# Attention steps moved by one chunk in a recurrent memory transformer, and memory transposes in 64-wide tiles

## The chip, the cores and the metric

The kernel runs on one core of one Trainium2 chip. The time is the device time of one execution in microseconds (us), lower is better. A run is given as the median of several executions, and one further execution was taken with the hardware profiler. The engines are called as in the profile: PE is TensorE (matmuls; PEld its weight loads), DVE is VectorE, ACT is ScalarE, POOL is GpSimd, SP is SyncE, which here only issues transfers.

## The reference, cut to what matters

Two independent halves are computed and joined along the last axis. Half A is a gated long convolution over 2048 positions and 1024 channels (done as a discrete Fourier transform by matmuls). Half B is a transformer layer with a recurrent memory, and all that is changed lies in it:

```python
mem = mem0                                  # 8 rows of 1024
for s in range(64):                         # 64 segments of 32 rows
    h = concat([mem, x[32*s:32*s+32]])      # 40 rows
    q, k, v = h @ Wq, h @ Wk, h @ Wv        # 32 heads of 128
    p = softmax(mask(q @ k.T * scale))      # memory columns are open, the rest causal
    o = (p @ v) @ Wo                        # 40 rows of 1024
    mem, out[s] = o[:8], o[8:]
```

Every segment needs the memory rows that the segment before it produced, so the 64 segments follow each other.

## The kernel before

At first half A runs, with matmuls of half B filled in: queries, keys and values of the last 8 rows of every segment, which need no memory, are computed for all segments at once and stored in DRAM (`REC`, `VBD`). Then comes the loop over 64 segments, which is most of the time. It is issued in an order written out by hand (`tc.manual_schedule()`): on each engine the instructions stand in the order in which the code calls them, and each waits for its inputs and buffers.

**Weights.** A chunk is 128 x 2048 bf16 (512 KB). Wq, Wk and Wv are 16 chunks each, Wo 16. Most stay in SBUF. The 14 that don't fit are read again in each segment through a ring of five slots (`wring`): `done(ch)` frees a slot as soon as the matmuls of its chunk have been recorded, and `fetch()` issues the next load on SP's queue (L722). Two further chunks of Wo, `KEPT_A` and `KEPT_B`, are held after the first segment in unused columns of PSUM: VectorE copies them in quarters into small SBUF tiles (`quarter`, `quarter_b`, L795) shortly before the matmuls that read them.

**A segment.** The 32 rows that depend on the memory or are not precomputed (8 of memory, 24 of x) go through six projections, `Proj(m, g)`: m is keys, queries, values; g is the first or second 16 heads. A projection has eight chunks, and a chunk is four matmuls (L938) that work on four column tiles of the array, 32 wide, each with 512 columns. `evac` (L947, ScalarE) copies the result to SBUF. Keys and queries are transposed on TensorE (L885 by 32-wide tiles, L957 by whole 128 x 128 blocks), then follow:

- `scores(g, ...)` (L963, L966) into the PSUM tile `SB`;
- `softmax_a` (row maximum L972 and difference L974 on VectorE, masks put back into SB L908 and L909 on VectorE, exponentials L977 on ScalarE);
- `softmax_b` (VectorE: sums L982, reciprocals and products, transposes L999 and L1000 into `PT`);
- `attend(g, PT, V)` (TensorE, L1007 and L1011) into the PSUM tile `OTp`, from 32-row tiles; `V` is the evacuated value projection;
- `evac_o(g)` (ScalarE, L1019), which copies `OTp` to the SBUF tile `OT`.

The output projection `out_half(hp, f, OT)` (L1029) takes one pair of heads hp and one half f of the columns: four matmuls of 256 columns in tiles 64 wide. `out_proj(hps, OT)` runs pairs for both halves. Pairs 0 to 7 belong to OT0, pairs 8 to 15 to OT1. The KEPT chunks are pairs 9 and 13 and come in quarters (`out_quarter`).

**The seam between segments.** The result goes to the SBUF tile `Y` in two halves of columns (L1118, ScalarE). `fill_mem(hT, Y, half)` turns the memory rows of each half with `turn_tile` (L885) into the PSUM tile `tps`, and VectorE copies them (L892) into the next segment's `rec`, the input of its projections. Half 0 is filled ahead of the last two pairs of output matmuls of the segment; half 1 stands behind the first four chunks of the next segment's first key projection.

**The order around the change** is the one in the code below: V0's projection `pv0`, the second scores, `softmax_a` for the second 16 heads (its exponentials included), three chunks of `pv1`, the first attention and its copy OT0, `softmax_b`, the other five chunks of `pv1`, the output projection of pairs 0 to 4, the second attention and its copy OT1, and pairs 5 to 7 as work ahead of the first user of OT1.

Of the kernel before, what the change touches and what calls it, by code (L numbers as in the profile page):

```python
# [420 lines left out]
def b_kernel(ctx: ExitStack, tc, x, mem0, Wq, Wk, Wv, Wo, outb, n_seg, run_a):  # L421
    nc = tc.nc
# [50 lines left out]
    ident = const.tile([128, 128], BF, name="ident")  # L473
# [263 lines left out]
    with c0p:  # L737
# [16 lines left out]
        for g in range(2):  # L754
# [3 lines left out]
            for tb in range(4):  # L758
                vst = vsts[:, tb] if g == 0 else pair()[:].rearrange("p (c w) -> p c w", c=4)
                for c in range(4):  # L760
                    ps = ps0.tile([128, 512], F32, tag="ps0", name="vb_ps")
                    for kc in range(8):
                        nc.tensor.matmul(ps[:], lhsT=xbt(kc)[:, 16 * tb:16 * tb + 16, :].rearrange("p s t -> p (s t)"),  # L763
                                         rhs=ws[kc][:, c * 512:(c + 1) * 512], start=(kc == 0), stop=(kc == 7))
# [115 lines left out]
        nc.gpsimd.dma_start(rec[:], REC[:, s, :])  # L880
        pend[s] = (rec[:, 0:256].rearrange("p (k t) -> p k t", k=8), rec[:, 256:512], rec[:, 512:768])

    def turn_tile(dst, src):
        for e in range(0, 128, 32):
            nc.tensor.matmul(dst[e:e + 32, :], lhsT=src[:, e:e + 32], rhs=ident[:], start=True, stop=True,  # L885
                             is_transpose=True, tile_position=(0, e))

    def fill_mem(hT, Y, half):
        tp = tps[:, 0, :]
        for j in (2 * half, 2 * half + 1):  # L890
            turn_tile(tp[:, j * 128:(j + 1) * 128], Y[:, j * 128:(j + 1) * 128])
        nc.vector.tensor_copy(  # L892
            hT.rearrange("p (dh j) t -> p dh j t", dh=2)[:, :, 2 * half:2 * half + 2, 0:NM],
            tp.rearrange("p (j dh r) -> p dh j r", j=4, dh=2)[:, :, 2 * half:2 * half + 2, 0:NM])

    with tc.manual_schedule():
# [3 lines left out]
        Y = one.tile([128, 512], BF, tag="PT", name="Y0")  # L900
# [6 lines left out]
        def seed_scores():  # L907
            nc.vector.tensor_copy(S[:, 0:4, :], mask[:, 0:1, :].to_broadcast([128, 4, 40]))  # L908
            nc.vector.tensor_copy(S[:, 4:8, :], mask[:, 1:2, :].to_broadcast([128, 4, 40]))  # L909
# [3 lines left out]
        for s in range(n_seg):  # L913
# [6 lines left out]
            def keys(g):  # L920
                KT = one.tile([128, 4, 4, 40], BF, tag="KT", name="KT")
                nc.gpsimd.tensor_copy(KT[:, :, :, 32:40],  # L922
                                      KBs[:, 128 * g:128 * g + 128].rearrange("p (c i t) -> p i c t", c=4, i=4))
                return KT
# [25 lines left out]
            def transposes(sb, tiles=False):  # L950
                tp = tps[:, 0, :]
                for i in range(4):
                    dst, src = tp[:, i * 128:(i + 1) * 128], sb[:, i * 128:(i + 1) * 128]
                    if tiles:
                        turn_tile(dst, src)
                    else:
                        nc.tensor.transpose(dst, src, ident[:])  # L957
                return tp.rearrange("p (i c r) -> p i c r", i=4, c=4)

            def scores(g, QT, KT):  # L960
                for i in range(4):
                    for c in range(4):
                        nc.tensor.matmul(S[32 * c:32 * c + 32, i, :], lhsT=QT[:, i, c, :], rhs=KT[:, i, c, :],  # L963
                                         start=False, stop=False, skip_group_check=True, tile_position=(0, 32 * c))
                for c in range(4):
                    nc.tensor.matmul(SB[32 * c:32 * c + 32, 160:320],  # L966
                                     lhsT=QBs[:, 128 * g + 32 * c:128 * g + 32 * c + 32], rhs=KT[:, :, c, :],
                                     start=False, stop=True, skip_group_check=True, tile_position=(0, 32 * c))

            def softmax_a():  # L970
                mx = two.tile([128, 8], F32, tag="mx", name="mx")
                nc.vector.tensor_reduce(out=mx[:], in_=S, op=ALU.max, axis=AX.X)  # L972
                E = one.tile([128, 8, 40], F32, tag="E", name="E")
                nc.vector.tensor_tensor(out=E[:], in0=S, in1=mx[:].unsqueeze(2).to_broadcast([128, 8, 40]),  # L974
                                        op=ALU.subtract)
                seed_scores()
                nc.scalar.activation(E[:], E[:], ACT.Exp, scale=scale)  # L977
                return E

            def softmax_b(E):  # L980
                ssum = two.tile([128, 8], F32, tag="ssum", name="ssum")
                nc.vector.tensor_reduce(out=ssum[:], in_=E[:], op=ALU.add, axis=AX.X)  # L982
                nc.vector.reciprocal(ssum[:], ssum[:])
                nc.vector.tensor_tensor(out=ssum[:, 4:8], in0=ssum[:, 4:8], in1=rowhead[:], op=ALU.mult)
                nc.vector.tensor_tensor(out=P_pad[:, 0:4, 0:32], in0=E[:, 0:4, 0:32],
                                        in1=ssum[:, 0:4].unsqueeze(2).to_broadcast([128, 4, 32]), op=ALU.mult)
                own = P_pad[:].rearrange("p b k -> p (b k)")[:, 32:320].rearrange("p (i w) -> p i w", w=72)
                nc.vector.tensor_tensor(out=own[:, 0:4, 0:8], in0=E[:, 0:4, 32:40],
                                        in1=ssum[:, 0:4].unsqueeze(2).to_broadcast([128, 4, 8]), op=ALU.mult)
                nc.vector.tensor_tensor(out=E[:, 4:8, :], in0=E[:, 4:8, :],  # L990
                                        in1=ssum[:, 4:8].unsqueeze(2).to_broadcast([128, 4, 40]), op=ALU.mult)
                nc.vector.tensor_copy(P_pad[:, 4, 32:64].rearrange("p (i t) -> p i t", i=4), E[:, 4:8, 32:40])
                with nc.allow_low_precision("one of the four terms is not zero"):
                    nc.vector.tensor_reduce(out=P_pad[:, 4, 0:32], in_=E[:, 4:8, 0:32].rearrange("p i k -> p k i"),
                                            op=ALU.add, axis=AX.X)
                PT = one.tile([128, 2, 4, 40], BF, tag="PT", name="PT")
                for kb in range(2):
                    ks = slice(32 * kb, 32 * kb + 32)
                    nc.vector.transpose(out=PT[:, kb, :, 0:32], in_=P_pad[:, 0:4, ks])  # L999
                    nc.vector.transpose(out=PT[:, kb, :, 32:40], in_=P_pad[:, 4, ks])  # L1000
                return PT
# [15 lines left out]
            def evac_o(g):  # L1017
                OT = one.tile([128, 4, 4, 40], BF, tag="KT" if g else "QT", name="OT")
                nc.scalar.copy(OT[:], o_view)  # L1019
                return OT  # L1020
# [12 lines left out]
            def out_half(hp, f, OT, stop=False):  # L1033
                w = pieces((3, hp, 0))
                for hh in range(2):
                    project(2 * hp + hh, f, w, OT, stop and hh == 1)
                if f == 1:
                    done((3, hp, 0))

            def out_proj(hps, OT):  # L1040
                for hp in hps:
                    for f in range(2):
                        out_half(hp, f, OT)

            def out_quarter(ch, q, w):
                project(2 * ch[1] + q // 2, q % 2, w, OT1)
# [15 lines left out]
            k1 = k1.run(4).evac()  # L1062
            scores(0, QT0, KT0)
            E0 = softmax_a()
            q1 = Proj(1, 1).run(4)
            KT1 = keys(1)
            nc.scalar.copy(KT1[:, :, :, 0:32], transposes(k1))
            PT0 = softmax_b(E0)
            q1 = q1.run(4).evac()
# [3 lines left out]
            V0 = pv0.run(4).evac()  # L1073
            scores(1, QT1, KT1)
            E1 = softmax_a()
            pv1 = Proj(2, 1).run(3)
            attend(0, PT0, V0)
            OT0 = evac_o(0)
            PT1 = softmax_b(E1)
            pv1.run(5)  # L1080
            if not last:
                load_x(s + 1)
            V1 = pv1.evac()
# [1 line left out]
            for f, hps in enumerate((FIRST, FIRST[-1:] + FIRST[:-1])):  # L1085
                for hp in hps:
                    out_half(hp, f, OT0)
            out_proj((4,), OT0)
            attend(1, PT1, V1)
            OT1 = evac_o(1)  # L1090
            qs = {}
            if s == 0:
                out_proj((5, 6, 7), OT0)
                out_proj((9, 13, 8), OT1)
                steps = {}
            else:
                qs["B", 0], qs["A", 0] = quarter_b(0, "E"), quarter(0, "rot")
                out_proj((5, 6, 7), OT0)
                qs["B", 2] = quarter_b(2, "QT")
                out_quarter(KEPT_B, 0, qs["B", 0])  # L1100
                qs["A", 2] = quarter(2, "E")
                out_quarter(KEPT_A, 0, qs["A", 0])
                qs["A", 1] = quarter(1, "rot")
                out_proj((8,), OT1)
                steps = {(0, 0): [("B", 2), ("B", 1, "QT")], (0, 1): [("A", 2), ("A", 3, "E")],
                         (0, 3): [("A", 1), ("B", 3, "rot")], (1, 0): [("B", 1)], (1, 1): [("A", 3)], (1, 2): [("B", 3)]}
            Y = one.tile([128, 512], BF, tag="PT", name="Y")
# [85 lines left out]
```

## Time and profile before

| | us |
|---|---|
| median of 3 runs | 1822.93 (1816.8 to 1824.99) |
| profiled execution, its own time | 1813.57 |
| its span, first to last instruction | 1811.8 |
| TensorE busy in the span | 1701.8 (94%) |
| VectorE, ScalarE, GpSimd busy | 1010.3, 680.7, 266.7 |
| mean granted TensorE clock | 0.985 |

The profiled execution lies below the median of the runs, and below the fastest of them; a difference is therefore added to each of the two. In the profile, a line of the timeline gives the start, the length (both in us), the engine, the source line with operation and tiles (written <- read), the shape, the number of instructions merged into it, and in brackets how long the engine was idle before it and what it waited for. The ends of matmuls are modelled, so that starts are the surer measure on TensorE. In a line of the windows the columns are the window, its length, the busy time of PE, PEld, DVE, ACT and POOL with instruction counts, the granted clock, the share of time in which DMA engines were busy, and GB/s moved.

### The profile page before, as it was taken

What the parts mean: (1) busy time and instruction counts of PE and PEld (TensorE: products, weight loads), DVE (VectorE), ACT (ScalarE), POOL (GpSimd) and SP (SyncE); (2) the same over time, 40 slices, a digit from 0 to 9 for tenths busy, and PEclk for the clock granted to TensorE, in tenths of its full rate; (3) what the DMA queues carried; (4) which work ended last, traced back from release to release, by engine and by line L of the source; (5) the groups of instructions that cost most, each with busy time, mean ns of one, the idle gap of its engine ahead of it and who ended that gap; (6) DMA issues with size and microseconds to landing.
All of it is one profiled execution on the core that took longest, in us unless ns stands there. A gap on an engine that the chain in (4) does not pass through costs nothing.

```text
span 1811.8 us, 71373 instructions
## 1 busy us (share of the span) xinstructions
PE 1701.8 (94%) x30996; PEld 1000.8 (55%) x31028; DVE 1010.3 (56%) x3391; ACT 680.7 (38%) x1195; POOL 266.7 (15%) x499
## 2 busy tenths in 40 slices
PE   6888996759899999999999999999999999999998
PEld 3443322324566666666666666666666666666665
DVE  9927874201455555555555555555555555555555
ACT  6955651112233333333333333333333333333333
POOL 4003341100111111111111111111111111111111
PEclk9999999889999999999999999999999999999999
DMA  9989889997999999999999999999999999999998
GB/s 340 370 305 305 311 258 320 306 335 210 344 365 361 357 350 360 358 363 353 361 356 358 357 352 360 370 358 360 361 355 362 356 358 366 367 363 356 357 358 300
DMA packets 233070, 623.34 MB, mean 344 GB/s; under 512 B 72802, under 2 KB 72946, under 8 KB 232756
## 3 DMA queue, kind: packets, MB, share of 16 engines
q1 hardware_dynamic: 160948, 550.58, 82.4%
q0 software_dynamic: 17056, 45.13, 7.1%
q10 hardware_dynamic: 54752, 23.07, 4.7%
q8 instruction: 243, 3.98, 0.9%
q14 instruction: 71, 0.58, 0.1%
HBM read 563.63 MB, written 57.67 MB: 343 GB/s over the span
## 4 chain that ended last, share of the span: by engine, by line
PE 77%; DMA 9%; DVE 6%; ACT 4%; issue 3%; ACTq 0%; POOL 0%; SPq 0%; another core or an unknown queue 0%; POOLq 0%; DVEq 0%
PE acc L938 33%; PE yacc L1029 24%; PE kb_ps L622 5%; DMA wring<-WS 4%; PE tps L885 3%; PE tps L957 2%; PE vb_ps L763 2%; ACT OT L1019 2%; DMA REC<-stage 2%; DVE mx L972 1%; DVE E L974 1%; ACT s_sb L247 1%; PE OTp L1007 1%; PE s_ps L245 1%; PE SB L963 1%
## 5 line engine op out<-in xcount | busy, mean ns | idle before, releaser
L1029 PEld LDWEIGHTS <-OT 128*64 128x64 bf16 x8255 | 439.1, 109 | 54.6 <-ACT OT L1019 36.9
L938 PEld LDWEIGHTS <-rec 128*32 128x32 bf16 x12288 | 289.4, 96 | 269.3 <-DVE rec L892 35.2
L947 ACT CAST qkv_sb<-acc 128x512 bf16<-128x512 f32 x384 | 225.1, 586 | 352.2 <-PE acc L938 346.9
L938 PE MATMUL acc<-Wres,rec 128*32 128x512 bf16 x3328 | 240.2, 382 | 2.0 <-issue 1.8
L938 PE MATMUL acc<-wring,rec 128*32 128x512 bf16 x2300 | 229.0, 382 | 8.5 <-DMA wring<-WS 7.3
L1029 PE MATMUL yacc<-Wmore,OT 128*64 128x256 bf16 (+1 forms) x2560 | 220.7, 274 | 0.0
L938 PE MATMUL acc<-Wmid,rec 128*32 128x512 bf16 x3072 | 212.1, 379 | 0.5 <-issue 0.3
L1029 PE MATMUL yacc<-wring,OT 128*64 128x256 bf16 x2448 | 194.9, 273 | 2.7 <-DMA wring<-WS 2.5
L1118 ACT CAST Y<-yacc 128x256 bf16<-128x256 f32 x128 | 47.7, 373 | 269.8 <-DVE quarter_b L795 170.8
L938 PE MATMUL acc<-pw,rec 128*32 128x512 bf16 x1796 | 144.7, 380 | 2.0 <-issue 1.9
L795 DVE TENSOR_SCALAR quarter<-OTp 128x256 int32<-128x256 int32 x252 | 99.9, 418 | 74.3 <-ACT OT L1019 74.3
L1019 ACT CAST OT<-OTp 128x640 bf16<-128x640 f32 x128 | 87.4, 683 | 138.5 <-PE OTp L1011 138.5
L1120 POOL DMA_DIRECT2D out_dram<-Y x128 | 63.9, 503 | 496.3 <-ACT Y L1118 496.0
L892 DVE COPY rec<-tps 128x32 bf16<-128x32 bf16 x128 | 22.4, 175 | 193.6 <-PE tps L885 193.6
L938 PE MATMUL acc<-Wlate,rec 128*32 128x512 bf16 x1536 | 117.3, 379 | 0.1
L1057 DVE COPY KT<-tps 128x512 bf16<-128x512 bf16 x64 | 27.2, 425 | 150.8 <-PE tps L885 150.8
L972 DVE TENSOR_REDUCE mx<-SB 128x8 f32<-128x320 f32 x128 | 63.0, 492 | 78.4 <-PE SB L966 78.4
L880 POOL DMA_DIRECT2D rec<-REC x64 | 36.4, 568 | 453.4 <-PE acc L938 437.9
L977 ACT ACTIVATE E<-E 128x320 f32<-128x320 f32 x128 | 60.1, 469 | 78.3 <-DVE E L974 78.3
L1029 PE MATMUL yacc<-Wlate,OT 128*64 128x256 bf16 x1024 | 79.2, 276 | 6.0 <-issue 0.2
L622 PE MATMUL kb_ps<-XBT,pw 128*128 128x512 bf16 x313 | 81.1, 397 | 2.6 <-DMA pw<-in_B_Wk_dram 1.2
L922 POOL COPY KT<-rec 128x128 bf16<-128x128 bf16 x128 | 38.5, 301 | 253.3 <-PE SB L966 253.3
(224 smaller groups left out, 2627.4 us busy)
## 6 DMA issues: line engine op xcount, KB each, us to landing
wring<-WS SPq DMA_DIRECT2D x831, 512.0 KB, 6.0
wring<-WS SPq DMA_DIRECT2D x64, 384.0 KB, 5.4
rec<-REC POOLq DMA_DIRECT2D x64, 192.0 KB, 5.6
SK<-s_sb SPq DMA_DIRECT2D x16, 512.0 KB, 5.3
SU<-s_sb SPq DMA_DIRECT2D x16, 512.0 KB, 5.6
Kg<-SK SPq DMA_DIRECT2D x32, 256.0 KB, 4.1
Ug<-SU SPq DMA_DIRECT2D x32, 256.0 KB, 5.5
REC<-stage ACTq DMA_DIRECT2D x16, 512.0 KB, 12.9
```

What stands on the lines that cost most here:

```text
L622: nc.tensor.matmul(ps[:], lhsT=ws[kc][:, hl * 128:(hl + 1) * 128], rhs=xbt(kc).rearrange("p s t -> p (s t)"), start=(kc == 0), stop=(kc == 7))
L795: nc.vector.tensor_scalar(out=dst, in0=src, scalar1=0, scalar2=None, op0=ALU.bitwise_or)
L885: nc.tensor.matmul(dst[e:e + 32, :], lhsT=src[:, e:e + 32], rhs=ident[:], start=True, stop=True, is_transpose=True, tile_position=(0, e))
L922: nc.gpsimd.tensor_copy(KT[:, :, :, 32:40], KBs[:, 128 * g:128 * g + 128].rearrange("p (c i t) -> p i c t", c=4, i=4))
L938: nc.tensor.matmul(self.acc[32 * c:32 * c + 32, :], lhsT=hT[:, ch[1], :], rhs=w[:, 512 * c:512 * c + 512], start=(ch == chs[0]), stop=(ch ...
L947: nc.scalar.copy(sb[:], self.acc[:])
L972: nc.vector.tensor_reduce(out=mx[:], in_=S, op=ALU.max, axis=AX.X)
L977: nc.scalar.activation(E[:], E[:], ACT.Exp, scale=scale)
L1019: nc.scalar.copy(OT[:], o_view)
L1029: nc.tensor.matmul(yacc[f][64 * dh:64 * dh + m, x - o:y - o], lhsT=lhsT, rhs=r, start=(h == (0, 2 * FIRST[-1])[f] and x == o), stop=stop, ...
L1118: nc.scalar.copy(Y[:, 256 * f:256 * f + 256], yacc[f][:, 0:256])
L1120: nc.gpsimd.dma_start(bass.AP(outb.tensor, outb.offset + SEG * s * 2048 + 512 * dh, [[2048, 32], [1, 512]]), Y[64 * dh + NM:64 * dh + 40, :])
```

## The change

Three edits. `turn_tile` gets a width, and half 0 of the memory is turned with four matmuls in tiles 64 wide instead of eight in tiles 32 wide; half 1 stays as it is. The exponentials leave `softmax_a` for a function of their own; for the first 16 heads they stay where they were, for the second 16 they are issued behind the first attention's copy OT0, and the first attention stands behind two chunks of `pv1` instead of three. The second attention stands behind pair 5 of the output projection instead of pair 4, so that pairs 6 and 7 are left between it and the first user of OT1.

```diff
-    def turn_tile(dst, src):
-        for e in range(0, 128, 32):
-            nc.tensor.matmul(dst[e:e + 32, :], lhsT=src[:, e:e + 32], rhs=ident[:], start=True, stop=True,
+    def turn_tile(dst, src, w=32):
+        for e in range(0, 128, w):
+            nc.tensor.matmul(dst[e:e + w, :], lhsT=src[:, e:e + w], rhs=ident[:], start=True, stop=True,
                              is_transpose=True, tile_position=(0, e))
 
     def fill_mem(hT, Y, half):
         tp = tps[:, 0, :]
         for j in (2 * half, 2 * half + 1):
-            turn_tile(tp[:, j * 128:(j + 1) * 128], Y[:, j * 128:(j + 1) * 128])
+            turn_tile(tp[:, j * 128:(j + 1) * 128], Y[:, j * 128:(j + 1) * 128], 32 if half else 64)
...
                 seed_scores()
+                return E
+
+            def softmax_exp(E):
                 nc.scalar.activation(E[:], E[:], ACT.Exp, scale=scale)
-                return E
...
             E0 = softmax_a()
+            softmax_exp(E0)
             q1 = Proj(1, 1).run(4)
...
             E1 = softmax_a()
-            pv1 = Proj(2, 1).run(3)
+            pv1 = Proj(2, 1).run(2)
             attend(0, PT0, V0)
             OT0 = evac_o(0)
+            softmax_exp(E1)
             PT1 = softmax_b(E1)
-            pv1.run(5)
+            pv1.run(6)
...
-            out_proj((4,), OT0)
+            out_proj((4, 5), OT0)
             attend(1, PT1, V1)
             OT1 = evac_o(1)
             qs = {}
             if s == 0:
-                out_proj((5, 6, 7), OT0)
+                out_proj((6, 7), OT0)
                 out_proj((9, 13, 8), OT1)
                 steps = {}
             else:
                 qs["B", 0], qs["A", 0] = quarter_b(0, "E"), quarter(0, "rot")
-                out_proj((5, 6, 7), OT0)
+                out_proj((6, 7), OT0)
                 qs["B", 2] = quarter_b(2, "QT")
                 out_quarter(KEPT_B, 0, qs["B", 0])
                 qs["A", 2] = quarter(2, "E")
                 out_quarter(KEPT_A, 0, qs["A", 0])
```

## The prediction

> **What bounds the kernel now.** I read the page first (busy time, slices, chain of waits), then the windows of the attention part, then the timeline of one undisturbed segment, since the change moves steps of 0.2 to 0.7 us that no total shows.
>
> ```profile
> PE 1701.8 (94%) x30996; PEld 1000.8 (55%) x31028; DVE 1010.3 (56%) x3391; ACT 680.7 (38%) x1195; POOL 266.7 (15%) x499
> PE 77%; DMA 9%; DVE 6%; ACT 4%; issue 3%; ACTq 0%; POOL 0%; SPq 0%; another core or an unknown queue 0%; POOLq 0%; DVEq 0%
> 1472.00:1638.80 166.80, 165.99 (x3660) 105.89 (x3659) 95.52 (x360) 60.26 (x112) 21.58 (x48) 1.00 0.98 364
> ```
>
> TensorE sets the end: 94% busy, 77% of the chain. The third line is a window of eight segments that nothing disturbed: 166.80 / 8 = 20.85 us each, TensorE busy 99.5% of it, the stream of weights at 364 GB/s. From the second copy into Y of the first segment (475.2 us) to that of the last (1807.5) the 63 segments take 21.15 us on average. So 20.85 is the floor of TensorE's own queue, and 0.30 per segment (19 us in all) is lost to late ring loads and to pauses that the profile calls issue. What the change costs must be read from TensorE's queue inside a clean segment. The first attention, in its timeline:
>
> ```profile
> 1482.68 0.59 ACT L947 CAST qkv_sb<-acc 128x512 bf16<-128x512 f32 x1 [0.46 <-PE acc L938]
> 1482.79 0.60 PE L938 MATMUL acc<-Wres,rec 128*32 128x512 bf16 x8
> 1483.33 0.27 PE L1007 MATMUL OTp<-PT,qkv_sb 32*128 32x40 bf16 x16
> 1483.44 0.23 PE L1011 MATMUL OTp<-PT,VBs 32*128 32x160 bf16 x4
> 1483.60 0.62 PE L938 MATMUL acc<-Wres,rec 128*32 128x512 bf16 x8
> 1483.88 0.47 ACT L977 ACTIVATE E<-E 128x320 f32<-128x320 f32 x1 [0.60 <-DVE E L974]
> 1484.25 0.67 ACT L1019 CAST OT<-OTp 128x640 bf16<-128x640 f32 x1
> 1484.26 0.60 PE L938 MATMUL acc<-Wres,rec 128*32 128x512 bf16 x8
> 1484.47 0.48 DVE L982 TENSOR_REDUCE ssum<-E 128x8 f32<-128x320 f32 x1
> 1484.98 0.30 PE L1029 MATMUL yacc<-Wlate,OT 128*64 128x256 bf16 x2
> ```
>
> The reader is to see two queues. On ScalarE the copy of V0 (L947) ends at 1483.27 and the attention starts 0.06 later; then the second exponentials (L977) stand ahead of the copy OT0 (L1019). On TensorE a chunk of four projection matmuls goes by in 0.215 us, start to start, when nothing waits, so the last two of pv1 end their issue at 1484.26 + 0.43 = 1484.69, and the output projection starts only at 1484.98, when OT0 (to 1484.92) is there. The second attention:
>
> ```profile
> 1486.84 0.17 DVE L1000 STREAM_TRANSPOSE PT<-P_pad 128x32 bf16<-128x32 bf16 x1
> 1487.28 0.27 PE L1007 MATMUL OTp<-PT,qkv_sb 32*128 32x40 bf16 x16
> 1487.74 0.69 ACT L1019 CAST OT<-OTp 128x640 bf16<-128x640 f32 x1 [2.18 <-PE OTp L1011]
> 1488.46 0.42 DVE L795 TENSOR_SCALAR quarter<-OTp 128x256 int32<-128x256 int32 x1 [1.15 <-ACT OT L1019]
> 1488.90 0.28 PE L1029 MATMUL yacc<-quarter_b,OT 128*64 128x256 bf16 x2
> 1489.01 0.28 PE L1029 MATMUL yacc<-quarter,OT 128*64 128x256 bf16 x2
> ```
>
> A chain hangs on this attention: OTp, the copy OT1 on ScalarE, behind it (1.15 us idle) the copy "quarter" of kept weights out of the same OTp on VectorE, and its use at 1489.01, only 0.13 after it ended (1488.88). Last, Y's transposes between output matmuls:
>
> ```profile
> 1491.84 0.27 PE L1029 MATMUL yacc<-B_rest,OT 128*64 128x256 bf16 x2
> 1491.90 0.22 PE L1029 MATMUL yacc<-quarter_b,OT 128*64 128x128 bf16 x1
> 1492.05 0.29 PE L885 MATMUL tps<-ident,Y 128*32 128x128 bf16 x8
> 1492.28 0.41 PE L1029 MATMUL yacc<-Wring,OT 128*64 128x256 bf16 x4
> 1492.45 0.17 DVE L892 COPY rec<-tps 128x32 bf16<-128x32 bf16 x1 [1.27 <-PE tps L885]
> 1492.83 0.40 PE L938 MATMUL acc<-wring,rec 128*32 128x512 bf16 x4
> ```
>
> **The price of a change of tile shape.** Output matmuls go by at 0.0545 us each. The row ahead of the second attention (four of them from 1486.97) would end its issue at 1487.19; the attention starts at 1487.28 though PT1 was ready at 1487.01. The first projection at 1492.83 follows four from 1492.52 (to 1492.74), and its rec was ready at 1492.62. So going to another tile shape costs 0.09 to 0.10 us with nothing to wait for.
>
> **Part 1, 64-wide transposes.** From 1491.84 the last kept weights, as much as two matmuls of 256 columns, 0.11 of issue, to 1491.95; transposes at 1492.05 (+0.10); eight of them to the next start 0.23, where the second half's eight, between 32-wide projections, take 0.11 (+0.12); the four output matmuls behind them 0.24 instead of 0.22 (+0.02). Four 64-wide tiles hold the same columns, two side by side instead of four, so their issue stays 0.11, and both changes of shape go: gain 0.24. The cover is then thin: transposes at 1491.95 end about 0.30 later, VectorE starts 0.11 behind that (as now), copies 0.17, and TensorE sees it 0.05 later: 1492.58; the projection would be due at 1491.95 + 0.11 + 0.44 + 0.10 = 1492.60. Were the copy late by a few hundredths, that much of the gain goes. The change of shape has no row for 64-wide transposes; between gain 0 and 0.24 I take 0.24, since the second half's rows show no cost of transposing itself.
>
> **Part 2, first attention one chunk earlier.** Two projection chunks stand ahead of it instead of three, so it is due at 1483.00 (1482.79 + 0.215), but V0 lands where it did: it starts at 1483.33 as before. The pause grows from 0.11 to 0.32, or, if the 0.06 behind V0 is chance and the 0.11 only the shape change, not at all. I take the pause: every copy of ScalarE that a matmul waits for is used 0.05 to 0.06 after its end (OT0: 1484.92 to 1484.98). Six chunks follow, 1483.60 + 6 x 0.215 + 0.02 + 0.10 for the shape = 1485.01. OT0 is no longer in the way: the attention's matmuls end at 1483.67, ScalarE takes 0.11 to see it (1487.63 to 1487.74 in the second), copies 0.69, done 1484.47. So 0.19 of waiting goes and 0.215 comes: the projection starts 0.03 later than now.
>
> **Part 3, the second exponentials behind OT0.** They start where the copy's end overlaps them by 0.10, at 1484.38 instead of 1483.88. Their reader L982 stood 0.12 behind their end, held by the second mask copy, so it slips 0.41 only, and with it the whole VectorE chain: PT1 at 1487.42. The second attention, 0.03 later and behind one more pair of heads (8 x 0.0545 = 0.44), is due at 1487.75. Cover 0.33: nothing lost. V1's copy, 0.2 later, still ends before the second half of the columns needs its accumulator.
>
> **Part 4, second attention one pair later.** Its chain moves with it by 0.47, but the users of OT1 and of "quarter" don't: two pairs of heads are left as cover instead of three. OT1: 1487.75 + 0.46 + 0.69 = 1488.90, just in time for quarter_b (due 1487.75 + 0.28 + 0.90 = 1488.93). "quarter" on VectorE: 1488.93 to 1489.35, usable at 1489.40; TensorE is due there at 1489.06. A new pause of 0.34; the matmuls now at 1489.01 start at 1489.40, 0.39 to 0.40 later. The later quarters queue behind on VectorE but slip only 0.17, so they gain cover. Queued behind that pause is all of TensorE: the rest of the output, Y, the next segment's projections. Of ring loads only those released after it (L722, pairs 8 and 14) are issued later.
>
> **Sum.** Per segment +0.40 - 0.24 = +0.16; over 63 segments +10 us. Against this, of the 19 us lost outside the floor some is given back, because a longer period gives each load more time: nothing at least, and at most what TensorE shows as waits for the ring, 7.3 + 2.5 = 9.8 us. I take 2, since such waits come in single bursts of up to 1 us, of which 0.16 buys back little. So +8: the profiled execution from 1813.57 to about 1821.6, the median from 1822.93 to 1831.
>
> **Rivals.**
> Stream-bound (no change, 1823): if the ring, not TensorE, sets the 21.15 average, a floor of 21.01 is still below it and nothing is seen. For it: DMA engines busy 97% to 98%, and 358 GB/s over the window of all 63 segments. Against it: eight segments in a row at 364 GB/s and the same 20.85. It decides from the point where the 0.30 lost per segment falls under 0.16. The Trainium skill, page "DMA: Bandwidth & Descriptors", section "Where 436 GB/s comes from", gives about 358 GB/s as the limit of one core's HBM side; by it a segment's 364 x 20.85 = 7.59 MB would need 21.2 us and the change would move nothing. The trace's mean agrees, its clean window does not.
> The first attention is not held by V0 (1818): it starts at 1483.11, everything behind is 0.21 earlier, and 63 x 0.21 = 13 us come off: 5 us faster than before. It decides if the first attention matmul starts more than 0.06 after V0's copy now because of the shape alone. The even 0.05 to 0.06 behind other ScalarE copies speaks against it.
> Transposes pay for shape at any width (1846): part 1 brings nothing, +15 us on top. The second half's 0.11 for eight speaks against it.
> The order not being as the edit says is excluded: in the built order TensorE, ScalarE and VectorE have these steps in these places, and the "quarter" copy waits for OT1's copy as before.
>
> **How the numbers follow.** Forecast 0.58, stream-bound 0.16, no V0 hold 0.08, no gain from width 0.10, something unlisted 0.08. The forecast's bounds are 1823 (all ring waits given back) and 1836 (none, and rec late by 0.05). The range 1819 to 1843 takes these in and leaves out most of the V0 and width cases. A measurement of this kernel tells about 0.5% (9 us) from no change; 1831 lies just within it, so the forecast gives 0.30 to slower and 0.28 to same; stream-bound and V0 give same 0.21 and faster 0.03; width is slower, 0.10; the unlisted go 0.05 to slower and 0.03 to faster.
>
> **What would show it.** In a clean segment after: period 21.0; first attention 0.05 to 0.06 behind V0's copy, 0.3 after TensorE was free; output projection not waiting for OT; "quarter" matmuls 0.05 behind VectorE's copy, with a TensorE pause of 0.3; transposes next to output matmuls at 0.11. A clean period at or under 20.85, or no pause at "quarter", would prove it wrong.

## The result and the profile after

The changed kernel takes 1830.83 us (median of 7 runs, 1829.04 to 1835.03) against 1820.06 for the kernel before in the same comparison: 11 us slower, ratio 1.0067 with a 95% interval of 1.0048 to 1.0087. The profiled execution took 1830.29 us, its span 1828.4. The forecast was 1831, from +8; the sign and the places were right, and part of the close hit is luck, since the three runs of before that it was added to lie 2 us above the median of 29 (1820.9): the difference itself was forecast as 8 us and measured as 11.

The page and a window of four undisturbed segments of the profile after, to be read against the busy times and the window shown of before:

```profile
PE 1708.5 (93%) x30772; PEld 997.2 (55%) x30772; DVE 1016.6 (56%) x3391; ACT 682.2 (37%) x1195; POOL 265.8 (15%) x499
1223.83:1308.00 84.17, 82.95 (x1816) 52.35 (x1816) 48.18 (x180) 30.26 (x56) 10.74 (x24) 1.00 0.97 359
```

TensorE is still the bound. A clean segment takes 84.17 / 4 = 21.04 us instead of 20.84, though over the whole run 256 matmuls fewer are issued, and TensorE idles 1.4% of it instead of 0.5%. The floor rose by 0.20 us, 63 x 0.20 = 12.6 us. The first attention in the timeline after:

```profile
1255.46 0.59 ACT L947 CAST qkv_sb<-acc 128x512 bf16<-128x512 f32 x1 [0.46 <-PE acc L938]
1255.57 0.39 PE L938 MATMUL acc<-Wres,rec 128*32 128x512 bf16 x4
1256.10 0.27 PE L1009 MATMUL OTp<-PT,qkv_sb 32*128 32x40 bf16 x16
1256.56 0.69 ACT L1021 CAST OT<-OTp 128x640 bf16<-128x640 f32 x1 [0.51 <-PE OTp L1013]
1257.14 0.47 ACT L980 ACTIVATE E<-E 128x320 f32<-128x320 f32 x1
1257.26 0.60 PE L938 MATMUL acc<-Wres,rec 128*32 128x512 bf16 x8
1257.79 0.52 PE L1031 MATMUL yacc<-Wlate,OT 128*64 128x256 bf16 x6
```

V0's copy ends at 1256.05 and the attention starts 0.05 later, as before; but only one chunk lies between 1255.57 and it, so TensorE pauses 0.53 - 0.215 = 0.32 us there. The copy OT0 is done at 1257.25, and the output projection at 1257.79 no longer waits for it: it follows its last eight matmuls by 0.53, which is 0.43 of issue and 0.10 for the change of tile shape. What the free copy gave, the longer pause took. The second attention:

```profile
1260.03 0.17 DVE L1002 STREAM_TRANSPOSE PT<-P_pad 128x32 bf16<-128x32 bf16 x1
1260.53 0.27 PE L1009 MATMUL OTp<-PT,qkv_sb 32*128 32x40 bf16 x16
1260.99 0.69 ACT L1021 CAST OT<-OTp 128x640 bf16<-128x640 f32 x1 [2.44 <-PE OTp L1013]
1261.71 0.43 DVE L795 TENSOR_SCALAR quarter<-OTp 128x256 int32<-128x256 int32 x1 [1.21 <-ACT OT L1021]
1261.73 0.30 PE L1031 MATMUL yacc<-quarter_b,OT 128*64 128x256 bf16 x2
1262.19 0.30 PE L1031 MATMUL yacc<-quarter,OT 128*64 128x256 bf16 x2 [0.16 <-DVE quarter L795]
```

PT1 is ready at 1260.20, 0.33 ahead of the attention: the late exponentials cost nothing here. Behind the attention the chain of copies ends at 1262.14, and the quarter's matmuls start 0.05 later, 0.46 behind those of quarter_b where 0.11 is their issue. The bracket gives 0.16 of idle time, because the ends of matmuls are modelled; the starts give 0.35. The list of TensorE's waits (total in us, how often, the longest in us) has it in all but two of the 63 segments that have quarters, and next the waits for the ring:

```profile
PE yacc L1031 <- DVE quarter L795: 9.6, 61, 0.2
PE acc L938 <- DMA wring<-WS: 8.2, 10, 5.2
```

And the seam:

```profile
1265.03 0.27 PE L1031 MATMUL yacc<-B_rest,OT 128*64 128x256 bf16 x2
1265.14 0.31 PE L885 MATMUL tps<-ident,Y 128*64 128x128 bf16 x4
1265.25 0.41 PE L1031 MATMUL yacc<-Wring,OT 128*64 128x256 bf16 x4
1265.47 0.42 PE L1031 MATMUL yacc<-pw,OT 128*64 128x256 bf16 x4
1265.54 0.17 DVE L892 COPY rec<-tps 128x32 bf16<-128x32 bf16 x1 [1.15 <-PE tps L885]
1265.81 0.40 PE L938 MATMUL acc<-wring,rec 128*32 128x512 bf16 x4
```

Start to start, the last kept weights, the transposes and twice four output matmuls behind them take 0.11, 0.11, 0.22 and 0.34, together 0.78, where it was 0.99 before (1491.84 to 1492.83). Both changes of shape around the transposes are gone. That this is 0.21 and not 0.24 has its cause further up in the segment; the last section comes back to it.

### The profile page after: what moved, and what is told of

Its sections match the earlier page's. It is cut to its first block, busy times and chain, and to the rows that moved or that the text cites. A ratio compares the mean times of both kernels' runs of the same rounds, so it can differ in the third digit from the quotient of the medians.

```text
span 1828.4 us, 70893 instructions
## 1 busy us (share of the span) xinstructions
PE 1708.5 (93%) x30772; PEld 997.2 (55%) x30772; DVE 1016.6 (56%) x3391; ACT 682.2 (37%) x1195; POOL 265.8 (15%) x499
## 4 chain that ended last, share of the span: by engine, by line
PE 76%; DMA 12%; DVE 5%; ACT 4%; issue 2%; POOL 0%; ACTq 0%; SPq 0%; POOLq 0%; DVEq 0%
PE acc L938 36%; PE yacc L1031 20%; DMA wring<-WS 6%; PE kb_ps L622 5%; PE tps L885 3%; PE tps L957 2%; PE vb_ps L763 2%; ACT OT L1021 2%; DMA REC<-stage 2%; DVE mx L972 2%; PE OTp L1009 2%; ACT s_sb L247 1%; DVE quarter L795 1%; PE s_ps L245 1%; DMA KS_nat<-in_A_ssm_k_dram 1%
## 5 line engine op out<-in xcount | busy, mean ns | idle before, releaser
L1031 PE MATMUL yacc<-wring,OT 128*64 128x256 bf16 x2448 | 199.7, 274 | 2.7 <-DMA wring<-WS 2.3
L1031 PE MATMUL yacc<-quarter,OT 128*64 128x256 bf16 x504 | 76.2, 275 | 9.7 <-DVE quarter L795 9.6
```

Source lines behind the costliest of these rows:

```text
L1031: nc.tensor.matmul(yacc[f][64 * dh:64 * dh + m, x - o:y - o], lhsT=lhsT, rhs=r, start=(h == (0, 2 * FIRST[-1])[f] and x == o), stop=stop, ...
```

## The experiments

Times are medians, each against the kernel before in the same comparison; "floor" is the length of a clean segment in the run's trace (with the last segment left out, the shortest fifth agree within 0.01 us). All floors can be compared, since TensorE's granted clock was full in the loop.

| kernel | floor, us | 63 x change of floor | measured | ratio to before, 95% interval |
|---|---|---|---|---|
| before | 20.84 | | 1820.9 | |
| changed | 21.04 | +12.6 | +10.8 | 1.0067 (1.0048 to 1.0087) |
| width_only | 20.605 | -15 | -12.1 | 0.9938 (0.9917 to 0.9959) |
| moves_only | 21.275 | +27 | +21.7 | 1.0123 (1.0098 to 1.0148) |
| three_chunks | 20.83 | -1 | -1.6 | 0.9998 (0.9982 to 1.0015) |
| pair8_first | 20.69 | -9 | -0.4 | 1.0004 (0.9989 to 1.0019) |
| second_unmoved | 20.705 | -8.5 | -0.8 | 0.9993 (0.9973 to 1.0014) |
| three_and_pair8 | 20.48 | -23 | -8.2 | 0.9946 (0.9926 to 0.9967) |
| second_one_more | 21.47 | +40 | +26.4 | 1.0151 (1.0128 to 1.0173) |

### The two halves of the change apart: width_only and moves_only

```diff
 # width_only: the kernel before, with
-            turn_tile(tp[:, j * 128:(j + 1) * 128], Y[:, j * 128:(j + 1) * 128])
+            turn_tile(tp[:, j * 128:(j + 1) * 128], Y[:, j * 128:(j + 1) * 128], 32 if half else 64)
 # moves_only: the changed kernel, with
-            turn_tile(tp[:, j * 128:(j + 1) * 128], Y[:, j * 128:(j + 1) * 128], 32 if half else 64)
+            turn_tile(tp[:, j * 128:(j + 1) * 128], Y[:, j * 128:(j + 1) * 128], 32)
```

> The kernel before with the 64-wide transposes of half 0 alone. Shape theory: two changes of tile shape go, clean segment 20.84 to about 20.63 us (the copy into rec, a few hundredths late, eats a little of the 0.24), so 63 x 0.21 = 13 us faster than before. Rival, stream-bound: the weights set the pace, clean segments may be shorter but the total stays within 3 us of before. Rival, transposes pay at any width: nothing.

> The changed kernel with half 0 turned in 32-wide tiles again, so only the moves of the attentions and of the exponentials. Pause theory: clean segment 21.045 + 0.21 = 21.25 us, 26 us slower than before, with the wait for the quarter copy in every segment. Stream-bound rival: the extra pauses are given back in part by fewer late loads, 15 us slower or less.

Measured: width_only 1808.79 us against 1820.94, floor 20.605, 0.235 less. moves_only 1842.62 us, floor 21.275, 0.43 more. So the 64-wide transposes are a gain of their own, and the moves are the whole loss. Both floors are as foretold to 0.03; of the times, width_only brought 12 of its 15 us and moves_only cost 22 of its 27. The expected loss of a few hundredths to a late copy into rec did not come: the whole 0.235 is there, and as much (21.275 - 21.04) lies between moves_only and the changed kernel.

### The pause at the quarter: pair8_first

```diff
                 qs["A", 2] = quarter(2, "E")
+                out_proj((8,), OT1)
                 out_quarter(KEPT_A, 0, qs["A", 0])
                 qs["A", 1] = quarter(1, "rot")
-                out_proj((8,), OT1)
```

> The changed kernel with pair 8 of the output projection recorded ahead of the first quarter of KEPT_A, so that 0.44 us of other matmuls lie between the second attention's copy chain and its user. Pause theory: the wait of 0.35 us at the quarter goes, clean segment 21.045 - 0.35 = 20.70 us, 9 us faster than before. If the 0.35 were anything else (a change of shape, a ring load of pair 8), it stays: 12 us slower than before.

The floor fell as the pause theory says, 0.35 to 20.69, and the wait for the quarter is gone from the list of TensorE's waits. The time fell by only half of that: 1820.51 us is some 11 us under the changed kernel, where the floor promises 22, and no faster than before (1820.94). What took the place of the pause stands in the same list, of this kernel:

```profile
PE acc L938 <- DMA wring<-WS: 16.9, 18, 5.4
```

16.9 us where the changed kernel waited 8.2. In both, about 6 us of it belong to the first segment; in the other 63, and with the waits in the output projection, it is 11.3 against 2.7. (The execution profiled took 1825.0 us, 4.5 more than the median, so the median may hold fewer of them.) The cause of the pause is shown; that taking it away makes the kernel faster than before is not.

### The first attention and V0: three_chunks

```diff
-            pv1 = Proj(2, 1).run(2)
+            pv1 = Proj(2, 1).run(3)
...
-            pv1.run(6)
+            pv1.run(5)
```

> The changed kernel with the first attention behind three chunks of pv1 again, five behind it; the copy OT0 stays ahead of the second exponentials. V0 theory: the attention starts at the same distance (0.05 us) behind V0's copy as in both kernels, one chunk less follows, clean segment 21.045 - 0.215 = 20.83 us, equal to before within 2 us. If the third chunk is paid wherever it stands: no change from the changed kernel, 12 us slower than before.

1819.34 against 1820.94, floor 20.83: 0.215 less than the changed kernel, as much as one chunk. In its trace the attention starts 0.057 behind V0's copy, as in the other two kernels. So moving the first attention up bought nothing at all: a chunk of waiting ahead of it in exchange for a chunk of work. The part that pays is the order of ScalarE's two instructions, OT0 ahead of the exponentials: with three chunks ahead of the attention in both kernels, the output projection starts 0.17 earlier in the segment here than before.

### The second attention: second_unmoved and second_one_more

```diff
 # second_unmoved: the changed kernel, with
-            out_proj((4, 5), OT0)
+            out_proj((4,), OT0)
...
-                out_proj((6, 7), OT0)
+                out_proj((5, 6, 7), OT0)
 # second_one_more: (4, 5, 6) ahead of the attention, (7,) behind it
```

> The changed kernel with the second attention back behind pair 4, three pairs as cover for its copies. Pause theory: no wait at the quarter, but PT1, 0.41 us late because of the exponentials behind OT0, is now waited for (due 15.22 us in the segment, ready and seen at 15.38): a wait of 0.16 in place of one of 0.35 and one of 0.03; clean segment about 20.83 us, equal to before within 2 us. If the late PT1 cost nothing: 20.66 us, 11 us faster.

> The changed kernel with the second attention moved by one more pair: behind pair 6, with pair 7 alone as cover for its copies. Pause theory: the wait at quarter_b grows from 0.03 to 0.47 us and the one at the quarter stays at 0.35, since OT1 is copied 0.44 later and nothing stands between; clean segment 21.48 us, 63 x 0.44 = 28 us slower than the changed kernel, 40 us slower than before less a fifth given back by the stream. If the pause had another cause than cover, no change from the changed kernel.

second_one_more behaves as the pause theory says: floor 21.47, 0.43 above the changed kernel, 1848.1 us. Of second_unmoved the time came as foretold (1819.91), but for another reason: the floor is 20.705, not 20.83. Its timeline shows why:

```profile
1126.96 0.17 DVE L1002 STREAM_TRANSPOSE PT<-P_pad 128x32 bf16<-128x32 bf16 x1
1127.25 0.17 DVE L1002 STREAM_TRANSPOSE PT<-P_pad 128x32 bf16<-128x32 bf16 x1
1127.31 0.27 PE L1009 MATMUL OTp<-PT,qkv_sb 32*128 32x40 bf16 x16
1127.47 0.25 PE L1013 MATMUL OTp<-PT,VBs 32*128 32x160 bf16 x4
```

The attention starts at 1127.31, though the last transposes of PT1 end at 1127.42. Its first 16 matmuls read only the first half of PT, which was ready 0.18 earlier (1127.13); only the four behind them wait, to 1127.47, and that costs 0.06 instead of 0.16 (from the attention's start to the first output matmul 0.34 instead of 0.28). So a late PT1 is cheap, and the second attention did not have to be moved for it. The 8.5 us promised by this floor did not come either, though pair 8 stands where it stood; so it was not the move of pair 8 alone that ate them.

### Less to stream: light_before, light_pair8_first, light_after, light_width_only

```diff
 # in fetch()
+            elif s > 0:
+                nc.sync.dma_start(t[:, 0:1536], stream_src(ch)[:, 0:1536])
             else:
                 nc.sync.dma_start(t[:], stream_src(ch))
 # in pieces(); Proj.run likewise reads columns 1024:1536 for its last 512
+        if now[0] > 0:
+            t = live[now[0], ch][1]
+            return [(0, 1536, t[:, 0:1536]), (1536, 2048, t[:, 1024:1536])]
```

From the second segment on, these kernels leave out the last quarter of each full ring load; the matmuls that would use it read columns 1024 to 1535 once more. So their output is not the reference's, and only the times count.

> The kernel before with less to stream: from the second segment on each ring load brings 1536 of its 2048 columns and the matmuls of the last 512 read columns 1024 to 1535 in their place, so the output isn't the reference's. Same matmuls, waits and order, 1.7 MB of 7.6 MB per segment less to move. If late ring loads make the time above the floor of 20.84 us, most segments come to 20.84 and the time falls by up to 19 us (20.84 x 63 in place of 21.15 to 21.3 x 63). If late instructions or engines make it, less than 5 us.

> The kernel of pair8_first with the same lighter ring loads. Stream theory: what the floor promised against before (20.69 against 20.84 us, 63 x 0.15 = 9 us) and pair8_first did not bring (0.7 us measured) was eaten by late loads, so here it is 9 us faster than light_before. Other theory: pair 8 placed earlier costs something of its own, and it equals light_before within 2 us.

> The changed kernel with the lighter ring loads (1536 of 2048 columns, the output isn't the reference's). Without late loads only TensorE's own queue is left: clean segments of 21.043 us everywhere, 63 x 0.20 = 12.6 us slower than light_before (1799.5), so about 1812. If part of the change's cost came from the stream, the difference is smaller here.

> The kernel of width_only with the lighter ring loads: clean segments of 20.605 us everywhere, 63 x 0.235 = 15 us faster than light_before, where width_only itself brought 11 to 12. If the transposes had helped the stream instead of TensorE's queue, it equals light_before.

| kernel with lighter loads | median, us | against light_before | 63 x change of floor |
|---|---|---|---|
| light_before | 1799.53 | | |
| light_after | 1809.61 | +10.1 | +12 |
| light_pair8_first | 1789.51 | -10.0 | -9 |
| light_width_only | 1784.04 | -15.5 | -15 |

Each is a median of four runs. light_after and light_width_only were timed in another comparison than light_before, in which the kernel before was 1.0 us longer (1821.75 against 1820.72), so that their differences are sure to about 1 us only.

Over light_before's whole loop the stream runs at 282 GB/s (last column):

```profile
477.50:1790.90 1313.40, 1306.37 (x28783) 829.16 (x28782) 751.86 (x2834) 474.12 (x882) 168.80 (x377) 1.00 0.86 282
```

1313.40 / 63 = 20.85: the segments are at their floor. The 0.30 us per segment above the floor go when the stream moves less, and most of the pauses called issue with them (in TensorE's projections they fall from 4.9 to 0.8 us). Here pair8_first brings the 10 us that it failed to bring with full loads, and width_only all of its 15. light_after is slower by 10.1 us in the medians and by 12.8 us in the loops of the two profiles, where its floor says 12: with lighter loads too, the change costs what its floor costs.

### Both pauses taken out: three_and_pair8

> The changed kernel with the first attention behind three chunks again and with pair 8 ahead of the first quarter of KEPT_A: both pauses that the change brought are gone, the 64-wide transposes and the free copy OT0 stay. By the floors: 21.043 - 0.215 - 0.351 = 20.48 us, 63 x 0.36 = 23 us faster than before. Stream-bound rival: the ring holds the average near 21.0 us whatever the floor, and it is no faster than width_only, some 11 us under before.

The edits of three_chunks and pair8_first together. The floor is 20.48, as summed; the time is 1812.49 us, 8 us under before and not below width_only. With full loads the loop runs at 359 GB/s, its segments 21.06 on average, 0.58 above the floor. Of the versions tried, width_only has the lowest median with full loads: 12 us under before, and so 23 us under the changed kernel. Its interval and that of three_and_pair8 overlap.

## Why the prediction was right

The four parts of its sum, one by one, against a clean segment (0.01 us resolution, starts only):

- Part 1, width: gain 0.24 foretold, 0.235 in width_only and 0.23 between moves_only and the changed kernel. The thin cover that the prediction named held (the last section has the rows).
- Part 2, first attention: the pause grew to 0.32 as foretold, and the projection of the output starts 0.04 later, foretold 0.03.
- Part 3, exponentials: nothing lost, as foretold. In the changed kernel the cover of 0.33 is there to the hundredth.
- Part 4, second attention: pause of 0.35 at the quarter, foretold 0.34, and 0.03 at quarter_b, where the copy OT1 was to be just in time. The matmuls of the quarter start 0.42 later in the segment, foretold 0.39 to 0.40.
- The sum per segment: +0.16 foretold, +0.20 measured. The sum lacks hundredths in parts 2 and 4 (0.02 in all) and one term, an echo of the pause at the quarter: 0.024 more from there to the end of the segment. The last section shows it.
- Give-back: 2 us were taken off. Against the floor's 12.6 us the medians say 1.8 us and the ratio (12 us, interval 9 to 16) leaves it open whether there was any. In moves_only the interval (18 to 27 us) just reaches the floor's 27; in second_one_more it is plain (23 to 32 of 40). The bound put on it was read from the wrong place: of the 9.8 us of ring waits, 7.8 lie ahead of 475.2, in the first segment, and only 2.0 in the 63 segments that lose the 19 us. Together with 5.8 us of issue the list names 7.8 us of these 19.
- The profiled execution was to take 1821.6 us and took 1830.29, 16.7 us more than that of before, twice the forecast. The one of before, 1813.57, lies 7 us under the median of its kernel, and the segments after lie 0.39 us above their floor on average instead of 0.31. That the median hit 1831 is luck to this extent: the forecast started 2.9 us above the median of before in the comparison, and its difference was 2.8 us too small.

Of the rivals, "not held by V0" fell by three_chunks and "no gain at any width" by width_only. "Stream-bound" fell as a forecast for this change: a longer floor is paid nearly in full. It holds in part for the other direction, which the prediction did not ask about: floors of 20.69 and 20.705 bring nothing, 20.48 brings 8 of 23 us, and the light runs of pair8_first and width_only show that it is the stream that takes the rest. The Trainium skill gives about 358 GB/s as the limit of one core's HBM side (page "DMA: Bandwidth & Descriptors", section "Where 436 GB/s comes from"). It is not a hard ceiling here, since clean segments ran at 364 and the loop of width_only at 360 GB/s on average. But near it TensorE waits for the ring (2.0 us in the loop of before, at 358 GB/s, and 7.7 in that of width_only), and in the loop of light_before, at 282, the list has no such wait.

Why width_only keeps 12 of its 15 us while pair8_first keeps almost none of 9, with like floors, is not settled. The profiles show only that the latter's ring waits are longer (11.3 against 7.7 us in the loop), with one profile each.

## What to carry to other kernels

Before a consumer is moved earlier, look at what released it: a step that starts 0.05 us behind a copy won't start sooner; the work moved out of its way is replaced by waiting. Before a producer is moved later, count the work left between the end of its chain of copies and the first user of each, here two pairs where three had just been enough. And where a stream of weights runs beside TensorE near its limit, a shorter queue on TensorE is worth what a run with full loads shows; a run with lighter loads tells how much more of it the stream holds back.

## What the hardware showed beyond that

Four 64-wide transposes between 64-wide matmuls cost only their issue, 0.11 us, while eight 32-wide ones there cost 0.33 to 0.35: 0.22 to 0.24 of it for the two changes of tile shape.

A pause on TensorE has a small echo. Output matmuls come in twos, one for each of the two 64-wide column tiles. Up to the quarter the two start 0.003 us apart in all kernels. In the kernels that wait at the quarter (changed, moves_only, three_chunks, second_one_more) they start 0.03 apart from there on, and the segment is 0.024 longer behind the quarter; in those without that wait (before, width_only, pair8_first, second_unmoved, three_and_pair8) they stay together. The 0.03 is paid at the next change of tile shape. With 64-wide transposes that is the first projection: the output matmuls behind the transposes take 0.563 to it instead of 0.536. In moves_only, whose transposes are 32 wide, it is paid ahead of them:

```profile
689.77 0.27 PE L1031 MATMUL yacc<-B_rest,OT 128*64 128x256 bf16 x2
690.00 0.29 PE L885 MATMUL tps<-ident,Y 128*32 128x128 bf16 x8
```

This is 0.23, where it is 0.21 before (1491.84 to 1492.05). So it is not a late copy into rec: in moves_only rec is ready 0.21 ahead of the projection and in the changed kernel 0.10, and in both, as in all the others, the projection starts 0.20 behind the last output matmul. Why the two column tiles stay out of step after the wait, no run here shows.
